# A fused adaLN block on one core: the last attention unit's keys in two halves with a running maximum, and the three-maxima mode from step 101 instead of 121

## The chip, the cores and the metric

The kernel runs on one core of a Trainium2 chip. The metric is the device time of one execution in microseconds (us): the median of three runs is 1090.26 us, and the runs lie between 1089.8 and 1090.3. The profile is of one more execution, which took 1090.18 us; its span, from the first profiled instruction to the last, is 1088.4 us. The engines are named as in the profile: PE (TensorE) multiplies matrices, DVE (VectorE) reduces and does elementwise work, ACT (ScalarE) does exponentials and copies, POOL (GpSimd) does elementwise work, and SP issues most DMAs.

## The reference, cut to what matters

```python
h = _layernorm(x) * (1 + ca) + sa
qkv = (h @ wqkv).reshape(B, S, 3, 16, 28)          # S = 2048, D = 448
scores = einsum("bhqd,bhkd->bhqk", q, k) * scale
p = softmax(scores)
x = x + ga * ((einsum("bhqk,bhkd->bhqd", p, v) -> B,S,D) @ wo)
h = _layernorm(x) * (1 + cb) + sb
x = x + gb * (gelu(h @ w1 + b1) @ w2 + b2)         # F = 1792
```

The weights are scaled up (wqkv and wo by 8, the MLP's by 64), so the scores are large: exp needs the row's maximum taken off first, and products are made of a rounded high part and a low part of each operand (three matmuls: high by high, low by high, high by low).

## The kernel before

**Tiling.** Four groups `g` of four heads by four blocks `qt` of 512 queries make 16 units `u = 4 * g + qt`. A unit has 16 steps, one for each 128 keys `kt`; `step = 16 * u + kt` runs from 0 to 255 (line 1355 on). In a step PE makes the scores of four heads, 12 matmuls (line 1393) into two PSUM tiles of two heads each; ACT takes exp of each tile (line 1406, two instructions in a step); and PE multiplies the step before's weights by V into the PSUM tile `o` (`av`, line 1348). `o` has one buffer for all units. V has a column of ones, so `o` also gathers the softmax's denominator.

**Maxima.** The row maximum of a unit is made ahead of the unit, from the high parts alone: for each unit 64 matmuls (4 sets of 128 queries, 4 heads, 4 chunks of 512 keys; `max_mm`, line 487), each reduced by DVE (`max_one`, line 492; two at once at line 698). `max_fin` (line 527) reduces the parts to one row maximum, and its `put` (line 535) turns them with a DVE transpose and writes them by four SP DMAs into row 28 of the unit's query tile `qst[u]`, where the first score matmul takes it off through a row of ones in K. All maxima of a unit have to be done by step 12 of the unit before it (`LAST_MAX`, line 34; `finish_max`, line 741). `mxq` holds the maxima still to do, in the units' order.

**Two modes.** Up to step 120 (`RING = 121`, line 35) a step emits 3 or 4 maxima as single matmuls between the score matmuls, and part of them as pairs whose difference goes through ACT (`open_pair` and `close_pair`, line 645 on). From step 121 on, a step emits three: a single one beside the first score tile (`emit_single`) and two with one DVE reduction beside the second (`emit_pair`). The two go into the PSUM tile that the next step's second score tile needs, so that tile waits for DVE's reduction. Once no maxima are left, the score tiles go round over three PSUM tiles (`three`, line 1366). Eight steps (8 to 11 of units 13 and 14, `is_wo`) also carry the output projection of an earlier query block and stay in the older mode.

**What runs beside the last steps.** From step 231 on, DVE and POOL make the second layernorm of block 0 (`ln2_stages`, line 1111; the calls are at lines 1287 to 1290): DVE statistics (lines 210, 211) and scaling (line 227), POOL products (lines 1130, 1131), a second round of statistics, a root on POOL (line 217), and four scalings, each with a short copy (line 1139). In steps 244 to 247 PE transposes the result (line 287) into the PSUM tile `m1`, ACT copies it (line 1198) and DVE makes the low part (line 1199). From step 245 on DVE prepares MLP weights that SP loads into `raw` (lines 1215 to 1228, 1236). At each unit's end ACT copies `o` out (line 1312); then come the denominator's reciprocal and its spread over the rows, with three SP DMAs (`den`, `drec`, `osb`, lines 1053 to 1063), two of which wait for the one ahead of them.

Instructions of one engine, and DMAs of one issuing queue, start in the order in which the program emits them, and each waits for what it needs: nothing is reordered.

## Time and profile before

| what | value |
|---|---|
| median of three runs (lowest, highest) | 1090.26 us (1089.8, 1090.3) |
| the profiled execution: time, span | 1090.18 us, 1088.4 us |
| granted TensorE clock | 1.00 over the span |
| DVE busy | 801.5 us, 74% |
| ACT busy | 696.8 us, 64% |
| POOL busy | 231.9 us, 21% |
| first exp of step 0 starts | 164.3 us into the span |
| last exp of step 255 ends | 790.1 us |

Times in what follows are microseconds from the start of the span of this profiled execution. The 256 steps of attention are found by the exp instructions of line 1406, two for each step. A busy PE says little, since matmuls overlap; a step's length says more.

### The profile page before, as it was taken

The numbers are of one execution on the slowest core, as the hardware profiler recorded it, in microseconds if no ns is written. First come the engines' busy times: TensorE is split into PE (matmuls) and PEld (weight loads), VectorE is DVE, ScalarE is ACT, GpSimd is POOL, SyncE is SP. The second block draws the span as 40 slices with busy tenths as digits, with TensorE's granted clock in tenths as the row PEclk, the third lists the DMA queues.
The fourth block names the chain that finished last, engine by engine and source line by source line (L and its number), as shares of the span: only waits on it lengthen the run. The fifth ranks groups of instructions, "written<-read, shape, count | busy, mean of one in ns | idle before, by whom it ended". The sixth has DMA issues, their size and how long they took to land.

```text
span 1088.4 us, 20665 instructions
## 1 busy us (share of the span) xinstructions
PE 1080.0 (99%) x8231; PEld 658.8 (61%) x8231; DVE 801.5 (74%) x1369; ACT 696.8 (64%) x883; POOL 231.9 (21%) x215
## 2 busy tenths in 40 slices
PE   8999999999999999999999999999999999999998
PEld 6766775444444444444444444544388888888887
DVE  6979788999999989988888988584745565464322
ACT  4665658888888888888888888687943321211211
POOL 1543330011011011024231410216114032061000
PEclk9999999999999999999999999999999999999999
DMA  9342272122121202143322423111343311002000
GB/s 312 134 155 76 86 208 88 41 67 58 50 78 59 77 28 58 56 120 87 103 68 77 131 65 96 58 31 59 117 126 96 102 37 41 33 35 73 34 1 34
DMA packets 58870, 88.56 MB, mean 81 GB/s; under 512 B 13807, under 2 KB 25734, under 8 KB 58762
## 3 DMA queue, kind: packets, MB, share of 16 engines
q1 hardware_dynamic: 58290, 86.51, 25.8%
q8 instruction: 64, 1.05, 0.4%
q10 hardware_dynamic: 148, 0.46, 0.1%
q0 software_dynamic: 336, 0.28, 0.1%
q14 instruction: 32, 0.26, 0.1%
HBM read 59.39 MB, written 29.50 MB: 82 GB/s over the span
## 4 chain that ended last, share of the span: by engine, by line
PE 98%; DMA 1%; DVE 1%; ACT 0%; issue 0%; SPq 0%; ACTq 0%
PE s L1393 24%; PE o L1348 24%; PE m L407 17%; PE pa L407 9%; PE m L487 8%; PE s L1485 3%; PE s L1487 3%; PE s L1486 3%; PE s L487 2%; PE t L1487 1%; PE t L1485 1%; PE t L1486 1%; DMA slot_c<-in_w_mod_dram 1%; PE o L287 1%; DVE mxp L492 0%; PE ma L487 0%
## 5 line engine op out<-in xcount | busy, mean ns | idle before, releaser
L492 DVE TENSOR_REDUCE mxp<-m 128x1 f32<-128x512 f32 x553 | 358.1, 686 | 65.0 <-PE m L487 47.7
L1393 PE MATMUL s<-slot_b,slot_a 28*128 28x512 f32 (+1 forms) x3072 | 357.8, 425 | 0.0
L1393 PEld LDWEIGHTS s<-slot_b,slot_a 28*128 28x128 f32 (+1 forms) x3072 | 210.7, 183 | 175.5 <-ACT slot_c L1406 96.4
L487 PE MATMUL m<-kh,qh 28*128 28x512 f32 x606 | 225.8, 469 | 0.8 <-DVE mxp L492 0.3
L1406 ACT ACTIVATE slot_c<-s 128x1024 f32<-128x1024 f32 x170 | 174.8, 1028 | 51.5 <-PE s L1393 50.5
L1348 PE MATMUL o<-slot_c,v 128*32 128x512 f32 x680 | 178.8, 605 | 0.0
L1441 ACT ACTIVATE full<-m,b_col 128x512 f32<-128x512 f32 x56 | 38.6, 690 | 194.2 <-PE m L407 190.0
L698 DVE TENSOR_REDUCE mxp<-s 128x2 f32<-128x1024 f32 x107 | 131.2, 1226 | 5.0 <-PE s L1393 0.3
L1348 PE MATMUL o<-slot_c1h,v 128*32 128x512 f32 x512 | 134.7, 605 | 0.0
L1348 PE MATMUL o<-slot_c0h,v 128*32 128x512 f32 x508 | 133.6, 605 | 0.0
L1406 ACT ACTIVATE slot_c0h<-s 128x1024 f32<-128x1024 f32 x127 | 130.7, 1029 | 0.0
L1406 ACT ACTIVATE slot_c1h<-s 128x1024 f32<-128x1024 f32 x128 | 130.7, 1021 | 0.0
L1406 ACT ACTIVATE slot_d<-s 128x1024 f32<-128x1024 f32 x86 | 88.4, 1028 | 26.1 <-PE s L1393 25.8
L487 PEld LDWEIGHTS m<-kh,qh 28*128 28x128 f32 x606 | 90.4, 182 | 15.4 <-DVE mxp L492 12.7
L1444 DVE CAST hi<-full 128x512 fp32r<-128x512 f32 x42 | 19.2, 458 | 102.0 <-ACT full L1441 101.9
L1068 POOL TENSOR_TENSOR osb<-osb,osb 128x512 f32<-128x512 f32 x16 | 20.6, 1285 | 343.6 <-DMA osb<-drec 282.3
L1348 PE MATMUL o<-slot_d,v 128*32 128x512 f32 x344 | 90.5, 605 | 0.4 <-ACT osb L1312 0.4
L1445 DVE TENSOR_TENSOR lo<-full,hi 128x512 fp32r<-128x512 f32 x56 | 46.2, 825 | 29.7 <-ACT hi L1444 25.7
L407 PE MATMUL m<-y,slot_a 128*128 128x512 f32 x160 | 59.7, 389 | 0.0
L662 DVE CUSTOM_DVE_ANT_0 slot_d0i<-m,slot_d0i 128x512 f32<-128x512 f32 x55 | 38.0, 691 | 16.6 <-PE m L487 14.3
L1348 PEld LDWEIGHTS o<-slot_c,v 128*32 128x32 f32 x680 | 24.5, 108 | 39.7 <-issue 37.8
L492 DVE TENSOR_REDUCE mxp<-ma 128x1 f32<-128x512 f32 x61 | 39.5, 681 | 11.6 <-PE m L487 7.2
(358 smaller groups left out, 1847.1 us busy)
## 6 DMA issues: line engine op xcount, KB each, us to landing
slot_b<-d SPq DMA_DIRECT2D x32, 256.0 KB
slot_a<-d SPq DMA_DIRECT2D x32, 256.0 KB
d<-lo SPq DMA_DIRECT2D x28, 256.0 KB
d<-hi SPq DMA_DIRECT2D x16, 256.0 KB
osb<-drec SPq DMA_DIRECT2D x15, 256.0 KB
out_dram<-xn SPq DMA_DIRECT2D x16, 224.0 KB
raw<-in_B_w_dram SPq DMA_DIRECT2D x14, 224.0 KB
qh<-d SPq DMA_DIRECT2D x12, 256.0 KB
```

Of the source, the lines that this page charges most:

```text
L407: pe.matmul(p, a, b, start=(i == 0), stop=(i == len(terms) - 1))
L487: pe.matmul(m, qh_sb[(g, qt)][js, i * 128 : (i + 1) * 128], k[js, :], start=True, stop=True)
L492: dve.tensor_reduce(out=mxp[(g, qt)][:, i, j, cch : cch + 1], in_=m, op=ALU.max, axis=AX.X)
L698: dve.tensor_reduce(out=mxp[(g, qt)][:, i, j : j + 2, cch], in_=t, op=ALU.max, axis=AX.X)
L1348: pe.matmul(o[32 * j : 32 * j + 32, :], v_sb[kt // 4][:, kt % 4, 4 * g + j, :], p[j // 2][:, j % 2, :], start=(kt == 0), stop=(kt == NKT - 1),
L1393: pe.matmul(s2[:, jj, :], ks[rows_, kp, kc], qs[rows_, qp, :], start=(term == 0), stop=(term == 2))
L1406: act.activation(pt[hf], s2, AF.Exp, scale=SCALE)
L1441: act.activation(gf, p, AF.Gelu_apprx_tanh, bias=b1_col[:, i : i + 1])
L1445: dve.tensor_tensor(out=glo, in0=gf, in1=f(ghi), op=ALU.subtract)
L1485: pe.matmul(pp, ghi[:, ts], w_hi, start=(m == 0), stop=False)
L1486: pe.matmul(pp, ghi[:, ts], w_lo, start=False, stop=False)
L1487: pe.matmul(pp, glo[:, ts], w_hi, start=False, stop=(m == NFT - 1))
```

## The change

Three things are done. `RING` goes from 121 to 101: twenty more steps run in the three-maxima mode. The last unit (`SPLIT`, unit 15) takes its keys in two halves: the maxima over its first 1024 keys are due where all were due before, those over the other 1024 keys by step 3 of the unit itself (`LAST_HALF`, step 243). The second half's score matmuls subtract a second row, the second maximum less the first, so the two halves have their own scale; the sum over the first half is set aside (`o1`), multiplied by exp of the difference of the maxima, and added at the end. For that `shift_exp` makes the factor on ACT and spreads it over the rows by five SP DMAs; a DVE copy empties `o` behind key step 7; POOL multiplies at step 252; and the unit's end adds on DVE where ACT copied. A buffer for descriptors is set to 8192 bytes. The maxima stay 1024 in all, the score and value matmuls the same in number.

```diff
-RING = 121
+RING = 101
+SPLIT = (NG - 1, NB - 1)
+HALF = NKT // 2
+LAST_HALF = NKT * (NG * NB - 1) + 3
...
+    w_dr = dr.tile([4, 512], F32, tag="w_dr", name="w_dr", bufs=1)
+    shift = {}
...
-    def max_fin(g, qt):
+    def max_fin(g, qt, cchs=slice(0, 4), row=0):
...
+        if row:
+            dve.tensor_tensor(out=m32[:, 0:16], in0=f(m32)[:, 0:16], in1=f(shift["m1"])[:, 0:16], op=ALU.subtract)
+        elif (g, qt) == SPLIT:
+            shift["m1"] = m32
         def put():
             r = sbt("full", [128, 512], F32R, bufs=3)[:, :32]
             dve.transpose(f(r), f(m32))
-            dst = f(qst[g * NB + qt])[DH:128:32, 0, :].rearrange("j (i b q) -> j i b q", b=4, q=32)
+            dst = by_block(f(qst[g * NB + qt])[DH + row : 128 : 32, 0, :])
             for b in range(4):
                 sp.dma_start(dst[:, :, b, :], f(r)[32 * b : 32 * b + 16, :])
+            if row:
+                shift["r"] = r
+                at(clock[0], shift_exp)
...
+    def shift_exp():
+        e = sbt("e32", [128, 32])
+        act.activation(e, f(shift["r"]), AF.Exp, scale=SCALE)
+        for b in range(4):
+            sp.dma_start(by_block(w_dr)[:, :, b, :], e[32 * b : 32 * b + 16, :])
+        shift["w"] = sbt("w1b", [128, 512])
+        sp.dma_start(shift["w"], w_dr[:, None, :].broadcast_to([4, 32, 512]))
...
+    def o_shift():
+        pool.tensor_tensor(out=shift["o"], in0=shift["o"], in1=shift["w"], op=ALU.mult)
+    at(last0 + 12, o_shift)
...
-        act.copy(o_sb, o)
+        if u < NU - 1:
+            act.copy(o_sb, o)
+        else:
+            dve.tensor_tensor(out=o_sb, in0=o, in1=shift["o"], op=ALU.add)
...
-                start=(kt == 0), stop=(kt == NKT - 1),
+                start=(kt == 0 or (u, kt) == (NU - 1, HALF)), stop=(kt == NKT - 1 or (u, kt) == (NU - 1, HALF - 1)),
...
+                if (pu, pkt) == (NU - 1, HALF - 1):
+                    shift["o"] = sbt("o1", [128, 512])
+                    dve.tensor_copy(shift["o"], po)
...
-            if kt == 0:
+            if kt == 0 or (u, kt) == (NU - 1, HALF):
                 o = ps_o()
...
-    nc = bacc.Bacc("TRN2", target_bir_lowering=False, num_devices=1)
+    nc = bacc.Bacc("TRN2", target_bir_lowering=False, num_devices=1, dynamic_dma_scratch_size=8192)
```

Left out of the diff are the bookkeeping of the two halves (`count`, `ready_max`, `finish_max`, `extra`) and the second subtracted row in the score matmul's slice (`n_shift`).

**PE, step 104.** The step in the order before and after: `s0`, `s1`, `s2` are the two-head PSUM tiles, `m1` and `m2` the single ones, `kh` and `qh` the high parts from which maxima are made. Before:

```order
L1393 MATMUL s1_1446_5852<-slot_b0_1242_5040,slot_a2_964_3930 128x512 x2
L487 MATMUL m2_1447_5855<-kh3_1185_4808,qh1_922_3767 128x512
L1393 MATMUL s1_1446_5852<-slot_b0_1242_5040,slot_a2_964_3930 128x512 x2
L487 MATMUL m1_1448_5860<-kh3_1185_4808,qh1_922_3767 128x512
L1393 MATMUL s1_1446_5852<-slot_b0_1242_5040,slot_a2_964_3930 128x512 x2
L1393 MATMUL s0_1449_5866<-slot_b0_1242_5040,slot_a2_964_3930 128x512 x6
L487 MATMUL m2_1450_5873<-kh2_1181_4788,qh1_922_3767 128x512
L487 MATMUL m2_1451_5876<-kh2_1181_4788,qh1_922_3767 128x512
```

After (line numbers are those of the changed kernel):

```order
L1444 MATMUL s1_1436_5836<-slot_b0_1242_5041,slot_a2_964_3931 128x512 x2
L490 MATMUL m1_1437_5839<-kh3_1185_4809,qh1_922_3768 128x512
L1444 MATMUL s1_1436_5836<-slot_b0_1242_5041,slot_a2_964_3931 128x512 x4
L1444 MATMUL s0_1438_5847<-slot_b0_1242_5041,slot_a2_964_3931 128x512 x4
L490 MATMUL s2_1439_5852<-kh2_1181_4789,qh1_922_3768 128x512 x2
L1444 MATMUL s0_1438_5847<-slot_b0_1242_5041,slot_a2_964_3931 128x512 x2
```

Four maxima matmuls in the step have become three, two of them into one tile and inside the second score group. Steps 101 to 120 all change in this way (their 79 maxima matmuls become 60). The 20 matmuls that leave steps 99 to 120 come back in steps 234 (one more), 235 (three, before none), 236 to 240 (three each, before none) and 241 (one).

**DVE, steps 237 and 238.** The layernorm's statistics (`st`, `mv`) and scaling (`xn`) of block 0, before:

```order
L210 BN_STATS st_10398<-xn_10320 128x6
L211 BN_AGGR mv_10397<-st_10398 128x2
L227 TENSOR_SCALAR xn_10401<-acc_17_101,mv_10137,rs_10281 128x448
L210 BN_STATS st_10427<-xn_10371 128x6
L211 BN_AGGR mv_10397<-st_10427 128x2
L227 TENSOR_SCALAR xn_10430<-acc_17_101,mv_10137,rs_10281 128x448
```

After:

```order
L495 TENSOR_REDUCE mxp_9655<-m_2398_10291 128x1
L733 TENSOR_REDUCE mxp_9655<-s_2400_10304 128x2
L213 BN_STATS st_10316<-xn_10230 128x6
L214 BN_AGGR mv_10315<-st_10316 128x2
L230 TENSOR_SCALAR xn_10319<-acc_17_101,mv_10030,rs_10182 128x448
L495 TENSOR_REDUCE mxp_9655<-m_2407_10328 128x1
L733 TENSOR_REDUCE mxp_9655<-s_2409_10341 128x2
L213 BN_STATS st_10352<-xn_10282 128x6
L214 BN_AGGR mv_10315<-st_10352 128x2
L230 TENSOR_SCALAR xn_10355<-acc_17_101,mv_10030,rs_10182 128x448
```

Each step's two reductions now stand ahead of its layernorm work. The same holds in steps 236, 239 and 240. Behind the last scaling of step 242 now stands the transpose of the second row, and behind the weights' third item (`raw`, step 247) the copy of `o`.

**SP, steps 242 to 246.** Before, from the loads of the first two weight rows:

```order
L1215 DMA raw_10551<-in_B_w_dram 128x512
L1215 DMA raw_10553<-in_B_w_dram 128x512
L1061 DMA drec_10616<-den_10522 128x16
L1063 DMA osb_10618<-drec_10616 128x1x512
L1215 DMA raw_10653<-in_B_w_dram 128x512
```

After:

```order
L1250 DMA raw_10495<-in_B_w_dram 128x512
L1250 DMA raw_10497<-in_B_w_dram 128x512
L553 DMA slot_b_2302_9846<-full_10499 4x4x32 x4
L564 DMA w_dr<-e_2449_10528 16x32 x4
L566 DMA w1b_10534<-w_dr 128x1x512
L1096 DMA drec_10574<-den_10466 128x16
L1098 DMA osb_10576<-drec_10574 128x1x512
L1250 DMA raw_10611<-in_B_w_dram 128x512
```

Nine DMAs have come ahead of unit 14's reciprocal and of the load of the third weight row, and three of the waits in this queue are now for landings that did not exist before or for DVE and ACT work of steps 242 and 243.

More of the change, by code (lines that the diff above doesn't have):

```diff
@@ L586, in count @@
                     load_hi(1, g + 1, cch)
-        if left[(g, qt)] == 0:
+        if (g, qt) == SPLIT:
+            before = first_left[0]
+            first_left[0] -= sum(cch < 2 for cch in cchs)
+            if before and not first_left[0]:
+                max_fin(g, qt, slice(0, 2))
+            if left[(g, qt)] == 0:
+                max_fin(g, qt, row=1)
+        elif left[(g, qt)] == 0:
             max_fin(g, qt)
@@ L607, in ready_max @@
     def ready_max():
-        return [m for m in mxq if there(1, m[0], m[2]) and there(0, *m[:2])][: 24 if clock[0] >= RING else 64]
+        near = [m for m in mxq if there(1, m[0], m[2]) and there(0, *m[:2])][: 24 if clock[0] >= RING else 64]
+        if near and clock[0] >= RING and NKT * (near[0][0] * NB + near[0][1] - 1) + LAST_MAX <= clock[0] + 8:
+            near = [m for m in near if m[:2] == near[0][:2] and (m[:2] != SPLIT or m[2] < 2 or not first_left[0])]
+        return near
     def by_set(m):
@@ L1331, in extra @@
         need = 0
[L1332 to L1334 removed]
+        ends = [(NKT * (v - 1) + LAST_MAX, left.get(divmod(v, NB), 64)) for v in range(s_ // NKT + 1, NU - 1)]
+        if s_ < NKT * (NU - 2) + LAST_MAX:
+            ends.append((NKT * (NU - 2) + LAST_MAX, first_left[0]))
+        if s_ < LAST_HALF:
+            ends.append((LAST_HALF, left.get(SPLIT, 64) - first_left[0]))
+        for end, n in ends:
+            need += n
+            rest = range(s_, end)
             n_wo = sum(is_wo(x) for x in rest)
```

19 lines of the change are left out of this document (11 added, 8 removed).

## The prediction

> **What bounds the kernel now.** I read the page's busy times and its chain of waits first.
>
> ```profile
> span 1088.4 us, 20665 instructions
> PE 1080.0 (99%) x8231; PEld 658.8 (61%) x8231; DVE 801.5 (74%) x1369; ACT 696.8 (64%) x883; POOL 231.9 (21%) x215
> ...
> PE 98%; DMA 1%; DVE 1%; ACT 0%; issue 0%; SPq 0%; ACTq 0%
> ```
>
> PE carries the chain from end to end and waits for almost nothing, so time is won only where a PE stretch gets shorter and lost wherever PE begins to wait. A busy PE does not tell how much it does, so the next view is the length of steps: windows over the exp instructions of line 1406, two to a step, each window from the end of one step's first exp to the end of a later step's first (the two exps cut by the edges are counted too).
>
> ```profile
> core 0: us, ACT busy (x), PEclk, DMA share, GB/s
> 419.66:469.90 50.24, 38.90 (x42) 1.00 0.19 58
> 521.70:557.80 36.10, 31.05 (x34) 1.00 0.35 101
> 748.77:756.75 7.98, 7.76 (x10) 1.00 0.20 78
> ```
>
> The first window is steps 101 to 120 in the older mode: 50.24 / 20 = 2.51 us a step. The second is the 16 steps of unit 9 in the three-maxima mode: 36.10 / 16 = 2.26. The third is steps 236 to 239, without maxima: 7.98 / 4 = 2.00. The clock is 1.00 in all three. So three maxima cost PE 0.26 us in the newer mode, 0.087 each, since they run beside score matmuls in other rows of the array.
>
> **Part 1, steps 101 to 120.** They go from 2.51 to 2.26 us: 20 x 0.256 = 5.1 us less; step 99 drops one matmul, which makes it **-5.2**. Nothing else moves to these steps. DVE does two reductions in place of three or four, and steps 121 to 233 keep their three maxima each.
>
> **Part 2, the twenty maxima that come back in steps 234 to 241.** On PE alone they cost 20 x 0.087 = 1.7 us. But DVE has the second layernorm to do there. Its timeline gives start, duration, line and tiles, and in brackets the idle time ahead and who ended it:
>
> ```profile
> start us, us, engine line op out<-in xcount [idle before <-releaser]
> 726.94 0.69 DVE L492 TENSOR_REDUCE mxp<-m 128x1 f32<-128x512 f32 x1 [0.34 <-PE m L487]
> 727.62 1.23 DVE L698 TENSOR_REDUCE mxp<-s 128x2 f32<-128x1024 f32 x1
> 728.76 0.62 DVE L210 BATCH_NORM_STATS2 st<-acc 128x6 f32<-128x448 f32 x1
> 729.41 0.18 DVE L211 BATCH_NORM_AGGREGATE mv<-st 128x2 f32<-128x6 f32 x1
> 729.51 1.85 DVE L492 TENSOR_REDUCE mxp<-m 128x1 f32<-128x512 f32 x3
> ...
> 751.24 0.63 DVE L210 BATCH_NORM_STATS2 st<-xn 128x6 f32<-128x448 f32 x1 [3.37 <-POOL xn L1131]
> 751.90 0.18 DVE L211 BATCH_NORM_AGGREGATE mv<-st 128x2 f32<-128x6 f32 x1
> 752.00 0.56 DVE L227 TENSOR_SCALAR xn<-acc,mv,rs 128x448 f32<-128x448 f32 x1
> ...
> 755.92 0.63 DVE L210 BATCH_NORM_STATS2 st<-xn 128x6 f32<-128x448 f32 x1 [1.48 <-POOL xn L1131]
> ...
> 756.80 0.17 DVE L215 TENSOR_SCALAR ve<-mv 128x4 f32<-128x4 f32 x1
> 758.10 1.33 DVE L227 TENSOR_SCALAR xn<-xn,mv,rs 128x448 f32<-128x448 f32 x1 [1.13 <-POOL rs L217]
> ...
> 763.42 0.51 DVE L227 TENSOR_SCALAR xn<-xn,mv,rs 128x448 f32<-128x448 f32 x1
> 763.96 0.20 DVE L1139 COPY xn<-xn 128x64 f32<-128x64 f32 x1
> ```
>
> Queued without a pause, instructions overlap a little: a single reduction takes 0.61 (1.85 for three) and a double one 1.14 (727.62 to 728.76), so a step's three maxima are 1.75 us of DVE. The layernorm work behind them is, by step: 236 a scaling, 0.5; 237 and 238 statistics and a scaling, 751.24 to 752.56 less the overlap, 1.24 each; 239 statistics, 0.84 (751.24 to 752.08); 240 the same and `ve`, 1.05 (755.92 to 756.97). That is 4.9, and with 5 x 1.75 it is **13.6 us of DVE in five steps** for which PE alone would take 11.3. Today DVE idles there and waits for POOL (the 3.37 and 1.48 in brackets). Afterwards POOL's two products of 1.15 each end well inside a DVE step of 3 us, and DVE is what is late. PE feels it directly: the second score tile of a step is the one that the step before's double reduction must have emptied.
>
> When does DVE start and what waits for its end? PE's timeline:
>
> ```profile
> 747.68 0.62 PE L1348 MATMUL o<-slot_c,v 128*32 128x512 f32 x2
> ...
> 765.14 0.66 PE L287 MATMUL m<-ident,xn 128*128 128x128 f32 x4
> ...
> 776.23 0.62 PE L1348 MATMUL o<-slot_c,v 128*32 128x512 f32 x2
> ```
>
> The scores of step 236 stand just ahead of the matmul of 747.68, so its first reduction can begin about 747.9, and 748.2 with the four maxima more of steps 234 and 235 (4 x 0.087). Add 13.6: `ve` ends at 761.8, where it ended at 756.97. The root on POOL takes 1.13 until DVE goes on (756.97 to 758.10), beside which the last single maximum and the two small operations on maxima fit: 763.0. The four last scalings and copies took 758.10 to 764.16, 6.06 us: 769.0. The new transpose adds 0.2, by the grouped rows of DVE (count, busy us, mean ns):
>
> ```profile
> L537 DVE STREAM_TRANSPOSE full<-m 128x32 f32<-128x32 f32 x1 | 0.2, 203 | 0.0
> ```
>
> So the second row is turned at 769.2. Two things hang on this. The first transposes of step 244 need all four scaled rows; they ran at 765.14, one microsecond behind DVE. And ACT's queue now holds `e32`, the exp of the turned row, ahead of the exps of step 244 (ACT's timeline):
>
> ```profile
> 764.24 1.02 ACT L1406 ACTIVATE slot_c<-s 128x1024 f32<-128x1024 f32 x1
> ...
> 791.42 0.20 ACT L1440 ACTIVATE full<-cst 128x1 f32<-128x1 f32 x1
> ```
>
> With `e32` at the price of the small activation of 0.20, step 244's exps start at 769.45 where they started at 764.24: **+5.2**. From there ACT has two exps of 1.02 and a copy in each step of 2.5 us, no room to catch up, so everything behind is later by that. This contains the 1.7 of PE. Bounds: 1.92 a step without overlap gives +6.1. If the last scalings ran at the 0.51 and 0.20 of their final pair, 2.8 in place of 6.06, it would be +1.9, little over PE's own price, and the sum 3.3 less.
>
> On that stretch a rule can be weighed. POOL's four additions lie beside it:
>
> ```profile
> 758.04 4.76 POOL L1161 TENSOR_TENSOR acc<-acc,row_b2g 128x448 f32<-128x448 f32 x4
> ```
>
> The scaling of 1.33 lies inside them, the one of 0.51 behind them. The Trainium skill, SBUF — State Buffer, section Who interferes with whom, says that a DVE operation in a two-port mode and a GpSimd operation take turns at a shared pair of ports, and the later one is fully blocked. The trace agrees (1.33 against 0.51). By the rule the stretch keeps its 6.06, since the additions again follow the root at once.
>
> **Part 3, the set-aside of `o`.** `o` has one buffer, so the first value matmul of the second half (step 249, 776.23 above) now waits for the DVE copy of `o`. In DVE's queue that copy stands behind the cast of the third weight row, and that row's load stands on SP behind nine new DMAs. The prices, from the timelines of SP and of DVE:
>
> ```profile
> 717.87 0.32 SPq L1061 DMA_DIRECT2D drec<-den  x1
> 720.40 0.54 SPq L1063 DMA_DIRECT2D osb<-drec  x1
> ...
> 742.67 2.27 SPq L540 DMA_DIRECT2D slot_b<-full  x4
> ...
> 767.56 0.33 SPq L1061 DMA_DIRECT2D drec<-den  x1
> 769.02 0.55 SPq L1063 DMA_DIRECT2D osb<-drec  x1
> 769.62 0.47 SPq L1215 DMA_DIRECT2D raw<-in_B_w_dram  x1
> ```
>
> ```profile
> 774.20 0.69 DVE L1199 TENSOR_TENSOR y<-m,y 64x512 fp32r<-64x512 f32 x1 [0.75 <-ACT y L1198]
> 775.30 1.18 DVE L1227 CAST slot_b<-raw 128x512 fp32r<-128x512 f32 x1 [0.40 <-DMA raw<-in_B_w_dram]
> 776.51 0.98 DVE L1228 TENSOR_TENSOR slot_a<-raw,slot_b 128x512 fp32r<-128x512 f32 x1
> ```
>
> From the turn at 769.2: four row DMAs 2.27, 771.5; four of `w_dr` between 0.33 and 0.57 each, taken as 0.45, 773.3; the wait for the last one's landing, 1.46 from its issue as for `drec` (767.56 to 769.02), 774.3; `w1b` 0.55, 774.9; `drec` and its landing, 776.4; `osb`, then the third row's load at 777.0. Its landing took 769.62 to 775.30, 5.68, with a broadcast just ahead as it has here: 782.6. Cast and difference 1.18 + 0.98, and the copy 0.69 (a 128x512 tile read from PSUM, as in the row of 774.20): 785.5. The matmul would be ready at 776.23 + 5.2 = 781.4. **+4.1.** Bounds: landing as fast as `drec`, 1.46, gives no wait at all; both write landings at the 2.5 of 717.87 to 720.40 and 0.57 for each `w_dr` give 6.7. I take the row of the very same load.
>
> The Trainium skill, DMA: Bandwidth & Descriptors, section Anatomy of one DMA, gives about 2.0 us of fixed cost to a DMA, for another issuing path than SP's. The trace shows 1.46 and 2.5 here. By the page's figure the two write landings would take 1.1 more together, an estimate, and the sum would be 1095.4.
>
> The rest costs nothing that PE sees. The second row lands by 773 and is needed at step 248, after 778: five microseconds of cover, and if it failed the price would be what it lacks. The factor's product on POOL and the addition at the end lie in front of a long MLP; DVE's addition takes the place of ACT's copy. The smaller descriptor buffer concerns three POOL DMAs behind the last step, which have the MLP as cover; I put it at 0, with at most a microsecond of SP-like issue time beside PE.
>
> **The sum.** -5.2 + 5.2 + 4.1 = +4.1 on the profiled 1090.18 (the median is 1090.26, 0.1 away): **1094.3 us**.
>
> **Rivals.** *The copy of `o` is in time* (the load lands in 1.5 us, or the chain on SP is shorter): -5.2 + 5.2, 1090.2, no change. It decides at a load that lands by 778.5. For it: the load is only 256 KB. Against it: 5.68 in the same place. *The layernorm doesn't hold PE, and the copy is in time, too*: only PE's 1.7 is paid, -5.2 + 1.7, 1086.7, **faster**. The mechanism is the last scalings running free of POOL's additions: then DVE turns the row near 766, where PE with 1.7 of delay arrives at 766.8 (765.14 + 1.7). It decides at 2.2 us less on DVE between 748 and 769. For it: each pair costs 0.71 when alone. Against it: the additions follow the root in POOL's queue. If only this half holds and the copy is late, it is 1090.8. *The change doesn't do what it says*: steps 101 to 120 stay at 2.51 because units 6 and 7 wait for loads that unit 9 did not: 1099.5. Against it: the score tiles, the queues and the number of maxima of a step are the same there as in unit 9.
>
> **How the numbers follow.** Chances: forecast 0.45, copy in time 0.25, both covered 0.18, only the scalings covered 0.07, no gain 0.05. The forecast's own range, with copy waits from 1.5 to 6.7, is 1091.7 to 1097. The range given, 1087.0 to 1097.0, takes in the cases of no change and half of the faster one; it leaves out the rest of that, the no-gain case and the upper tail, under 0.2. A measurement tells 0.2%, 2.2 us, from no change: faster 0.22 (both covered, and a part of the second case), same 0.30, slower 0.48.
>
> **What would show it.** Step length near 2.26 in steps 101 to 120 (part 1). In steps 236 to 240, DVE without idle time and PE's second score tile released by the double reduction; steps near 3 us (part 2). A PE gap ahead of step 244's transposes, released by DVE, and ACT idle ahead of `e32`. At step 249 a PE gap at the first value matmul, released by the DVE copy, with that DVE waiting for `raw`'s DMA (part 3). The prediction is wrong if the layernorm's scalings end within 2 us of where they ended, counted from step 236, or if step 249 has no gap.

## The result, and the profile after

The changed kernel takes **1100.34 us** (median of five runs, 1099.78 to 1101.9), the kernel before took 1089.95 beside it: a ratio of 1.0097, 95% interval 1.0083 to 1.0111. The forecast was 1094.3 in a range of 1087.0 to 1097.0: the sign was right, the size was less than half of what came. Ranges and intervals, here and below, leave out two executions that took far longer than all others of their kernel, 1942.88 us of `both` and 1618.89 us of the kernel before beside both_adds, both_exp and best2. The profiled execution of the change took 1100.62 us. From its page, the span, the busy times, the slices of PE and of its granted clock (40 slices of 27 us), and the chain of waits:

```profile
span 1098.8 us, 20650 instructions
PE 1081.7 (98%) x8231; PEld 657.1 (60%) x8231; DVE 809.7 (74%) x1350; ACT 692.6 (63%) x873; POOL 232.8 (21%) x216
...
PE   8999999999999999999999999999799999999998
PEclk9999999999999999999999999999899999999999
...
PE 96%; DMA 2%; DVE 1%; ACT 1%; issue 0%; SPq 0%; ACTq 0%
```

The busy times hardly moved. One slice stands out: the 29th, where PE is at 7 and its clock at 8. It lies at 769 to 797 us, the last steps of attention. To see where the time goes, take from ACT's timeline of each trace the end of every step's first exp, and subtract:

| end of the first exp of step | before, us | after less before, us | what lies between |
|---|---|---|---|
| 101 | 419.69 | -0.38 | |
| 121 | 469.90 | -5.49 | part 1: -5.1 |
| 198 | 644.71 | -5.45 | |
| 200 | 649.14 | -4.16 | +1.3, not foreseen |
| 234 | 739.84 | -4.30 | |
| 240 | 756.79 | -2.49 | part 2, first half: +1.8 |
| 244 | 765.26 | -0.17 | part 2, second half: +2.3 |
| 249 | 777.19 | -0.39 | part 2 in all: +3.9 |
| 250 | 779.26 | +9.23 | part 3: +9.6 |
| 251 | 781.19 | +10.53 | part 3 in all: +10.9 |
| 255 | 789.19 | +10.53 | |

The span differs by 10.44. Part 1 is there: windows over the exps, cut as in the prediction, give 45.13 / 20 = 2.26 us a step in steps 101 to 120 (2.51 before). The second window is steps 236 to 239, 2.40 us a step where they took 2.00.

```profile
419.28:464.41 45.13, 38.86 (x42) 1.00 0.21 65
744.70:754.30 9.60, 7.88 (x9) 1.00 0.17 66
```

Part 2 on DVE: the first reduction of step 236, `ve`, the first of the four scalings and the turn of the second row. POOL's additions (the last line, from POOL's timeline) run beside the scalings:

```profile
743.21 0.69 DVE L495 TENSOR_REDUCE mxp<-m 128x1 f32<-128x512 f32 x1 [2.26 <-PE m L490]
...
756.43 0.17 DVE L218 TENSOR_SCALAR ve<-mv 128x4 f32<-128x4 f32 x1
...
757.74 1.34 DVE L230 TENSOR_SCALAR xn<-xn,mv,rs 128x448 f32<-128x448 f32 x1
...
763.70 0.21 DVE L550 STREAM_TRANSPOSE full<-m 128x32 f32<-128x32 f32 x1
```

```profile
757.67 4.75 POOL L1196 TENSOR_TENSOR acc<-acc,row_b2g 128x448 f32<-128x448 f32 x4
```

Part 3 begins on SP. Its timeline after the turn of the second row (start, duration, tiles, count):

```profile
763.94 2.26 SPq L553 DMA_DIRECT2D slot_b<-full  x4
766.30 1.79 SPq L564 DMA_DIRECT2D w_dr<-e  x4
769.14 0.56 SPq L566 DMA_DIRECT2D w1b<-w_dr  x1
769.80 0.42 SPq L1096 DMA_DIRECT2D drec<-den  x1
774.35 0.55 SPq L1098 DMA_DIRECT2D osb<-drec  x1
774.95 0.47 SPq L1250 DMA_DIRECT2D raw<-in_B_w_dram  x1
```

`osb` reads what `drec` wrote, so SP waits for `drec`'s landing: 769.80 to 774.35, 4.55 us, where the same pair took 1.46 before. DVE's and PE's timelines show the rest, the cast that waits for the row, the copy behind it, and the value matmul that waits for the copy:

```profile
780.80 1.33 DVE L1262 CAST slot_b<-raw 128x512 fp32r<-128x512 f32 x1 [6.29 <-DMA raw<-in_B_w_dram]
782.16 0.98 DVE L1263 TENSOR_TENSOR slot_a<-raw,slot_b 128x512 fp32r<-128x512 f32 x1
783.17 0.69 DVE L1467 COPY o<-o 128x512 f32<-128x512 f32 x1
```

```profile
783.91 1.07 PE L1396 MATMUL o<-slot_c,v 128*32 128x512 f32 x2 [8.01 <-DVE o L1467]
```

The matmul takes 1.07 us where it took 0.62. Windows tell why (length; busy time and count of PE, PEld, DVE, ACT, POOL; then the granted clock, the share of the DMA engines and GB/s):

```profile
770.00:776.00 6.00, 5.91 (x60) 2.67 (x58) 2.99 (x5) 5.83 (x8) 0.00 (x0) 1.00 0.17 52
776.00:779.95 3.95, 0.00 (x0) 0.00 (x0) 0.00 (x0) 1.71 (x2) 0.00 (x0) 1.00 0.83 223
780.05:790.20 10.15, 6.29 (x36) 2.13 (x40) 9.13 (x13) 1.94 (x2) 4.94 (x4) 0.50 0.39 128
790.30:792.00 1.70, 1.70 (x22) 0.58 (x18) 1.63 (x4) 1.31 (x2) 0.00 (x0) 1.00 0.77 248
```

Four us into PE's idle time the granted clock falls to 0.50, and it stays there for 10.2 us, 6.3 of them after PE has begun again. Half of 6.3 is 3.1 us of lost clock, close to the 2.9 that steps 249 to 251 lost beside the 8.0 of waiting (10.9 less 8.0).

The +1.3 at step 198 goes with a wait of PE for DVE that the kernel before doesn't have there:

```profile
639.38 0.50 PE L490 MATMUL s<-kh,qh 28*128 28x512 f32 x1 [0.78 <-DVE mxp L495]
```

Three single reductions follow one another there; `emit_pair` found no two neighbours among the few maxima that the new rule in `ready_max` leaves it close to a due time.

### The profile page after: what moved, and what is told of

Read it like the earlier page. It is cut to its first block, busy times and chain, and to the rows that moved or that the text cites. A ratio compares the mean times of both kernels' runs of the same rounds, so it can differ in the third digit from the quotient of the medians.

```text
span 1098.8 us, 20650 instructions
## 1 busy us (share of the span) xinstructions
PE 1081.7 (98%) x8231; PEld 657.1 (60%) x8231; DVE 809.7 (74%) x1350; ACT 692.6 (63%) x873; POOL 232.8 (21%) x216
## 4 chain that ended last, share of the span: by engine, by line
PE 96%; DMA 2%; DVE 1%; ACT 1%; issue 0%; SPq 0%; ACTq 0%
PE s L1444 24%; PE o L1396 23%; PE m L410 16%; PE pa L410 9%; PE m L490 7%; PE s L1539 3%; PE s L1541 3%; PE s L1540 3%; PE s L490 2%; PE t L1541 1%; PE t L1539 1%; PE t L1540 1%; DMA slot_c<-in_w_mod_dram 1%; PE o L290 1%; DVE mxp L495 1%; DMA raw<-in_B_w_dram 1%
## 5 line engine op out<-in xcount | busy, mean ns | idle before, releaser
L495 DVE TENSOR_REDUCE mxp<-m 128x1 f32<-128x512 f32 x523 | 340.6, 686 | 72.9 <-PE m L490 55.2
L1444 PE MATMUL s<-slot_b,slot_a 28*128 28x512 f32 (+2 forms) x3072 | 358.7, 426 | 0.1
L1444 PEld LDWEIGHTS s<-slot_b,slot_a 28*128 28x128 f32 (+2 forms) x3072 | 211.4, 184 | 186.9 <-ACT slot_c L1457 106.2
L490 PE MATMUL m<-kh,qh 28*128 28x512 f32 x566 | 215.5, 470 | 0.8 <-DVE mxp L495 0.3
L733 DVE TENSOR_REDUCE mxp<-s 128x2 f32<-128x1024 f32 x131 | 160.6, 1226 | 5.8 <-PE s L1444 0.5
L490 PEld LDWEIGHTS m<-kh,qh 28*128 28x128 f32 x566 | 85.5, 182 | 13.3 <-DVE mxp L495 10.7
L490 PE MATMUL s<-kh,qh 28*128 28x512 f32 x264 | 59.0, 438 | 0.8 <-DVE mxp L495 0.8
```

Source lines behind the costliest of these rows:

```text
L490: pe.matmul(m, qh_sb[(g, qt)][js, i * 128 : (i + 1) * 128], k[js, :], start=True, stop=True)
L495: dve.tensor_reduce(out=mxp[(g, qt)][:, i, j, cch : cch + 1], in_=m, op=ALU.max, axis=AX.X)
L733: dve.tensor_reduce(out=mxp[(g, qt)][:, i, j : j + 2, cch], in_=t, op=ALU.max, axis=AX.X)
L1444: pe.matmul(s2[:, jj, :], ks[rows_, kp, kc], qs[rows_, qp, :], start=(term == 0), stop=(term == 2))
```

## The experiments

Thirteen kernels, each beside the kernel before on the same chip. "Gap" is PE's idle time ahead of step 249's first value matmul.

| kernel | median, us (lowest, highest) | ratio to before, interval | gap, us |
|---|---|---|---|
| the change | 1100.34 (1099.78, 1101.9) | 1.0097 [1.0083, 1.0111] | 8.0 |
| copy_first | 1097.22 (1096.94, 1099.31) | 1.0067 [1.0054, 1.0080] | none |
| spread_late | 1095.45 (1094.46, 1095.94) | 1.0044 [1.0029, 1.0060] | 3.2 |
| split_only | 1096.34 (1094.47, 1097.11) | 1.0053 [1.0039, 1.0067] | 1.9 |
| ring_only | 1098.07 (1097.71, 1099.39) | 1.0074 [1.0062, 1.0087] | none |
| both | 1090.64 (1089.39, 1093.7) | 1.0005 [0.9996, 1.0014] | none |
| pool_queue | 1095.03 (1094.49, 1095.58) | 1.0043 [1.0029, 1.0057] | 3.9 |
| keep_busy | 1099.17 (1098.2, 1100.11) | 1.0081 [1.0067, 1.0095] | 1.0 |
| best1 | 1089.42 (1088.23, 1090.41) | 0.9991 [0.9982, 1.0000] | none |
| both_adds | 1090.62 (1089.22, 1091.82) | 1.0003 [0.9994, 1.0013] | none |
| both_exp | 1090.0 (1089.12, 1091.52) | 1.0001 [0.9992, 1.0010] | none |
| best2 | 1088.24 (1087.45, 1088.72) | 0.9982 [0.9973, 0.9991] | none |
| spray_w1b | 1098.56 (1097.31, 1099.61) | 1.0082 [1.0067, 1.0097] | 7.0 |
| spray_both | 1096.8 (1096.26, 1097.95) | 1.0070 [1.0053, 1.0087] | 4.9 |

**copy_first: the copy ahead of the late cast.**

```diff
-        at(last0 + 5 + k + (k >= 4), w_prep.step)
+        at(last0 + 5 + k + (k >= 2), w_prep.step)
```

> The changed kernel, with the weight preparation's third and fourth items one step later each (steps 248 and 249 in place of 247 and 248), so that the DVE copy of o stands ahead of the cast that waits for the late weight load. Theory: the wait at step 249 is the copy standing behind that cast, and the slow TensorE clock of the next steps comes from PE's idle time. Then the 8.0 us gap and the 2.8 us of slow clock go: 1100.3 - 10.9 = 1089.4 us, granted clock 1.00 throughout. Rival 1: the late load itself holds PE, if not there then where the weights are first used: the time stays above 1097 us with a new gap near 790 us. Rival 2: the slow clock has another cause: the gap goes and the time is about 1092.3 us.

The gap at step 249 is gone: the offset against before is +0.6 from step 245 to step 255. But the time is 1097.22, not the 1089.4 of the theory. Most of the loss came back some 20 us later, in the MLP's projection, as PE's timeline shows (the profiled execution, 1099.31, is the slowest of the five; the others lie below 1097.3):

```profile
800.75 0.44 PE L410 MATMUL m<-slot_e,slot_c 128*128 128x448 f32 x1 [3.22 <-DMA slot_c<-o]
803.22 0.71 PE L410 MATMUL m<-slot_e,slot_c 112*128 112x448 f32 x1 [2.03 <-DMA slot_c<-o]
```

Behind the first of these waits the granted clock is 0.50 again, from 802.7 to 809.4. SP issues the loads of `slot_c` at 797.35; before it did at 789.34. So removing the wait at PE doesn't heal the queue that was late: it moves the wait to the next reader of that queue. The rival had this mechanism, if with other loads.

**spread_late: the broadcast of `w1b` five steps later**, behind `drec` instead of ahead of it.

```diff
+        at(clock[0] + 5, shift_spread)
+
+    def shift_spread():
         shift["w"] = sbt("w1b", [128, 512])
```

> The changed kernel, with the spread of the factor over the rows (the broadcast DMA into w1b) issued at step 248, behind the weight loads, in place of step 243. Theory: drec's landing took 4.55 us from its issue because the broadcast was in the DMA queues ahead of it. Then it takes about 1.5 us, the third weight row's load is issued 3.6 us earlier (3.05 for the landing and 0.6 for the broadcast's issue), and PE's gap at step 249 goes from 8.0 to about 4.4 us: 1096.7 us if the clock falls as before, about 1094 us if the shorter gap keeps it. Rival: drec's landing is slow for another reason, and it stays near 4.5 us: 1099.7 us.

SP's timeline: from `drec`'s issue to `osb`'s are 1.48 us now, not 4.55.

```profile
768.67 0.37 SPq L1099 DMA_DIRECT2D drec<-den  x1
770.15 0.56 SPq L1101 DMA_DIRECT2D osb<-drec  x1
```

The gap fell from 8.0 to 3.2 (forecast 4.4), and still cost 5.85 in steps 249 to 251: the clock's price, 2.7, stayed.

**both: the two edits together.**

> Both single edits together: the set-aside copy of o stands ahead of the casts of the third weight row, and the broadcast of w1b is issued in step 248 instead of behind w_dr. Theory (all of the late loss comes from SP's queue: the copy behind a late cast, and drec's landing behind the broadcast's packets): the reciprocal's DMA lands in about 1.2 us instead of 4.5, the gap of 8.0 us ahead of step 249's value matmuls is gone as in copy_first, and the projection's loads (slot_c<-o) come early enough that the gaps of 3.2 and 2.0 us near 800 are gone too; what is left is -5.1 +1.3 +3.9 = about 0, so 1089 to 1091. Rival (the eight small DMAs of SP, four slot_b and four w_dr, make the tail's loads late by themselves): gaps of 2 to 5 us near 795 to 805 stay, 1093 to 1096.

It came out nearly as the theory had it: `drec` to `osb` 1.50 us (forecast 1.2), no gap at step 249, none near 800, and a span 0.3 us under that of before. Part 3 is thus two things together: SP's queue, late behind the broadcast, and the copy's place on DVE behind the cast that waits for SP's load (split_only, below, has the second alone). What is left is -5.1 + 1.3 + 3.9 = 0.1. The smaller descriptor buffer was not tried alone, but from step 255 (-0.23) to the end of the span (-0.3) `both` loses nothing, so the prediction's 0 for it holds here.

**split_only and ring_only: one part of the change alone.** split_only leaves `RING` at 121; ring_only is the kernel before with `RING = 101`.

> The changed kernel with RING back at 121: the split of the last unit without the longer three-maxima mode. All maxima are done by step 234, as before the change; the second row is turned about step 235, and its nine DMAs are through before unit 14's reciprocal. Theory: nothing of the layernorm is held up, and the third weight row lands as it did before the change; what is left is the copy of o behind its cast: 775.3 + 1.18 + 0.98 + 0.69 = 778.2 where the matmul could start at 776.2, a gap of 2 us: 1092 us. Rival: the split itself (its nine DMAs, the second row, the extra DVE and POOL work) costs more by itself: 1094 us or above.

> The kernel before with RING at 101 and nothing else: the last unit isn't split, and 20 steps between 108 and 227 carry a fourth maximum to keep the old due time. Theory: steps 101 to 120 give 5.1 us, and the fourth maximum costs what a step of the older mode costs over one of the newer, 0.25 us, since DVE then has about 2.4 us of reductions in a step of 2.26: 20 x 0.25 = 5.0 us, 1089.9 us, no change. Rival: a fourth maximum costs PE's 0.087 us alone, 1.7 us in all: 1086.5 us, faster, and the split was not needed for the gain.

split_only has no late maxima, since they are made by step 234, and its offset stays at +1.0 from step 235 to 249, so part 2's loss needs the late maxima. It took 1096.34 where its theory had 1092. The theory's gap is there (1.86 us, forecast 2), but two terms were not in it. At step 212 three single reductions stand in a row again, PE waits 0.78 us for DVE, and the offset goes from -1.0 to +1.0 by step 215. And the clock drops even for a gap of 1.86, 1.3 us after PE has begun again and for 3.4 us (windows as above):

```profile
779.15:780.49 1.34, 1.34 (x12) 0.47 (x16) 1.31 (x2) 0.00 (x0) 1.34 (x2) 1.00 0.60 171
780.49:783.90 3.41, 3.41 (x24) 1.08 (x20) 3.31 (x6) 1.94 (x2) 0.43 (x1) 0.50 0.40 120
783.90:785.00 1.10, 1.10 (x20) 0.35 (x12) 1.07 (x3) 0.39 (x1) 0.00 (x0) 1.00 1.06 401
```

Its median lies 1.9 us above its profiled execution; that difference is not explained. ring_only shows what the split is for: without it the twenty maxima must come back by step 235. In the trace sixteen of them are a fourth one in a step (108, 116 and fourteen steps from 124 to 227), and the other four stand in steps 234 and 235. Its offset goes from -2.96 at step 121 to +8.86 at step 231, 11.8 / 14 = 0.84 us for each, where the theory had 0.25 and the rival 0.087: both failed. One of PE's waits for DVE there:

```profile
619.05 0.50 PE L487 MATMUL m<-kh,qh 28*128 28x512 f32 x1 [0.85 <-DVE mxp L492]
```

**pool_queue: the nine DMAs on POOL's queue.**

```diff
-                sp.dma_start(dst[:, :, b, :], f(r)[32 * b : 32 * b + 16, :])
+                (pool if row else sp).dma_start(dst[:, :, b, :], f(r)[32 * b : 32 * b + 16, :])
...
-            sp.dma_start(by_block(w_dr)[:, :, b, :], e[32 * b : 32 * b + 16, :])
+            pool.dma_start(by_block(w_dr)[:, :, b, :], e[32 * b : 32 * b + 16, :])
...
-        sp.dma_start(shift["w"], w_dr[:, None, :].broadcast_to([4, 32, 512]))
+        pool.dma_start(shift["w"], w_dr[:, None, :].broadcast_to([4, 32, 512]))
```

> The change as it is, but the second row's four DMAs, the four of w_dr and the broadcast of w1b are issued by POOL instead of SP; the copy of o stays behind the cast. Theory (it is their place in SP's queue that makes the third weight row, its cast, the copy and the projection's loads late): SP is in time as before, drec's landing about 1.5 us, the gap ahead of step 249's value matmuls under 1 us, no lower granted clock behind it, no gaps near 800: about 1090.2 (-5.1 +1.3 +3.9). Rival 1 (the landing of drec is slow because the broadcast's packets load the DMA engines, whatever queue they come from): drec still lands 3 us or more later than it was issued, the gap at step 249 stays at 2 to 4 us and the clock drops: 1094 to 1096. Rival 2 (POOL, which waits for e32 and then issues, holds its own copies and scalings): new waits on POOL's tiles, over 1094 without a wait for osb.

SP is in time (`drec` to `osb` 1.44 us, the third row's load issued at 767.54), and yet a gap of 3.9 us stays. Gap and time are those of the first rival, but its late `drec` is not there. POOL waits 5.20 us for `w_dr`, and its own work then falls on DVE's cast (DVE's timeline, then POOL's):

```profile
773.32 3.19 DVE L1262 CAST slot_b<-raw 128x512 fp32r<-128x512 f32 x1 [0.36 <-DMA raw<-in_B_w_dram]
776.55 0.98 DVE L1263 TENSOR_TENSOR slot_a<-raw,slot_b 128x512 fp32r<-128x512 f32 x1
777.56 0.69 DVE L1467 COPY o<-o 128x512 f32<-128x512 f32 x1
```

```profile
773.14 0.71 POOL L566 DMA_DIRECT2D w1b<-w_dr  x1 [5.20 <-DMA w_dr<-e]
773.86 1.15 POOL L1196 TENSOR_TENSOR acc<-acc,row_b2g 128x448 f32<-128x448 f32 x1
774.96 1.26 POOL L1103 TENSOR_TENSOR osb<-osb,osb 128x512 f32<-128x512 f32 x1
```

Such a cast takes 0.42 at 770.37, while POOL waits, and this one 3.19 beside three instructions of POOL. The theory missed this; the second rival had the place (POOL held up) but not the way in which it cost.

The run also bears on part 2, by accident. POOL makes only two of its four additions before it comes to the new DMAs, and DVE's scalings are short as soon as those two end (POOL's timeline, then DVE's):

```profile
757.19 2.39 POOL L1196 TENSOR_TENSOR acc<-acc,row_b2g 128x448 f32<-128x448 f32 x2
```

```profile
757.25 1.33 DVE L230 TENSOR_SCALAR xn<-xn,mv,rs 128x448 f32<-128x448 f32 x1
...
759.56 0.50 DVE L230 TENSOR_SCALAR xn<-xn,mv,rs 128x448 f32<-128x448 f32 x1
```

The stretch of scalings is 4.4 us instead of 6.05, the second row is turned in time for `e32`, which waits for nothing, and between steps 242 and 244 nothing is lost (-2.09 to -2.06).

**keep_busy: matmuls in the gap.** 64 score matmuls that nothing reads stand ahead of step 249's value matmuls.

```diff
+                if (pu, pkt) == (NU - 1, HALF):
+                    busy = ps_s2()
+                    for n in range(64):
+                        rows_ = slice(32 * (n % 2), 32 * (n % 2) + DH)
+                        pe.matmul(busy[:, n % 2, :], ks[rows_, 0, kc], qs[rows_, 0, :], start=n < 2, stop=n >= 62)
```

> The change as it is, and 64 more matmuls of the score form into a free score buffer just ahead of step 249's value matmuls, in place of part of the 8.0 us wait (by the rows of step 251, where a pair starts every 0.2 us, they take about 6.4 us); nothing reads them. Theory (the granted clock falls because PE idles for 8 us): the wait left is about 1.6 us, the windows behind it show a granted clock near 1.0, the value matmuls of step 249 take 0.62 us instead of 1.07, steps 249 to 251 are 2 to 3 us shorter and the time falls to 1097 to 1098.5 although PE does more. Rival (the clock falls for another reason, such as the matmuls' own load): the value matmuls stay near 1.07 us and the time stays at 1100.3 or goes over it.

PE's timeline and the window behind the gap:

```profile
785.03 0.62 PE L1396 MATMUL o<-slot_c,v 128*32 128x512 f32 x2 [0.96 <-DVE o L1472]
```

```profile
784.00:788.00 4.00, 3.04 (x32) 0.89 (x30) 3.90 (x6) 0.96 (x2) 2.80 (x2) 1.00 0.20 57
```

The clock is 1.00, the value matmuls take 0.62, and steps 249 to 251 lose 8.6 us instead of 10.9, though PE does more. The time fell by 1.2 only, to 1099.17 where the forecast was 1097 to 1098.5; in the profiled pair 0.6 went to a later start of step 0 (+0.1 against -0.5). That idling is what takes the clock is shown.

**both_adds and both_exp: what part 2's second half is.** both_adds moves POOL's additions four stages later in the program, both_exp moves `e32` to step 248 (and the broadcast to 249, its use to 253).

```diff
-                (t, 4 + t, 6 + t, 10 + t // 2, 10 + t),
+                (t, 4 + t, 6 + t, 10 + t // 2, 14 + t),
```

```diff
-                at(clock[0], shift_exp)
+                at(clock[0] + 4, shift_exp)
```

> both, and POOL's additions to block 0 four stages later (t of 14 to 17 instead of 10 to 13), nothing else. Theory A (in steps 242 to 244 the loss comes from DVE's scalings and copies that run beside POOL's additions and are three times as long): the stretch of scalings shrinks from 6.06 us to 2.8 to 4.7 and the offset against before at step 244, 0.0 in both, falls to -1.3 to -2.0: 1088.5 to 1089.2. Theory B (the loss comes from e32, which holds ACT's queue until the second row is turned, whatever the scalings last): the offset at step 244 stays within 0.4 of both's and the time at 1090.5.

> both, and e32 with its w_dr DMAs four steps later (step 248), the broadcast in step 249 and its use in step 253, nothing else. Theory A (long scalings beside POOL's additions hold DVE; ACT waits because it is behind them): e32 no longer holds ACT, but PE then waits for DVE itself or not at all: offset at step 244 from 0.0 to -0.3 at most if DVE was what PE waited for. Theory B (only e32's place on ACT makes a late turn of the row cost anything): the stretch of scalings stays at 6.06 us, the offset at step 244 falls by 1.3 us or more: about 1089.

both_adds moved nothing on the chip. POOL has nothing else to do there, so it reaches the additions at the same time as before, and DVE's scaling is as long as ever (POOL's timeline, then DVE's):

```profile
757.91 1.02 POOL L220 TENSOR_TENSOR rs<-ve,cst 128x4 f32<-128x4 f32 x1 [2.78 <-DVE ve L218]
758.90 4.76 POOL L1199 TENSOR_TENSOR acc<-acc,row_b2g 128x448 f32<-128x448 f32 x4
```

```profile
758.96 1.34 DVE L230 TENSOR_SCALAR xn<-xn,mv,rs 128x448 f32<-128x448 f32 x1
```

So it says nothing on theory A; pool_queue, above, does. both_exp settles the other side: between steps 242 and 244 the offset moves by 0.0 (-1.36 to -1.35) where `both` lost 1.5 (-1.46 to 0.00), with the scalings as long as they were. So the 1.5 us need both: the long scalings, which turn the second row late, and `e32`'s place in ACT's queue, which holds the exps until then. pool_queue takes away the first, both_exp the second, and either is enough. The time doesn't show the gain: the span of both_exp is 1088.2 us, that of `both` 1088.1, because the projection, whose loads of `slot_c` SP issues no earlier (790.67 against 790.48), gives back what steps 242 to 244 won; the forecast of about 1089 was missed by 1.0. The other 2.7 us (-4.06 at step 234 to -1.36 at step 242 in both_exp) stay. split_only, without the late maxima, loses nothing there; best2, below, with the layernorm moved away, still loses 1.2, near the 1.7 that the prediction had for the maxima on PE alone. So some 1.5 of the 2.7, by the difference of best1 and best2, are DVE's, which carries late maxima and layernorm together. In the change the row of `e32` was:

```profile
763.94 0.23 ACT L562 ACTIVATE e<-full 128x32 f32<-128x32 f32 x1 [1.31 <-DVE full L550]
```

**spray_w1b and spray_both: why a small DMA lands late behind a broadcast.** In the change, the DMA view of 771 to 773 us, when only `w1b`'s packets run (busy tenths of the 16 DMA engines in 40 slices, then packets, MB and share):

```profile
DMA  2142222332232323313323143132331431323314
...
q1 hardware_dynamic: 97, 0.20, 26.0%
```

Only a quarter of the engines is busy, and of `drec`'s 128 packets 96 had gone by 770.9 while 32, a quarter, came at 773.1 to 773.7. The edit makes one DMA for each of the four source rows; spray_both does the same for unit 14's `osb`, just ahead of the third weight row.

```diff
-        sp.dma_start(shift["w"], w_dr[:, None, :].broadcast_to([4, 32, 512]))
+        for j in range(4):
+            sp.dma_start(shift["w"][32 * j : 32 * j + 32, :], w_dr[j][None].broadcast_to([32, 512]))
```

> The change as it is, but the broadcast of w1b is four DMAs, one for each row of w_dr onto 32 partitions, instead of one whose source has 4 rows of 32 copies. Theory (the one broadcast runs on 4 of the 16 DMA engines, since 32 of drec's 128 packets, 4 engines' share of 16, came 2.4 us after the other 96; drec waits for those four): the packets of w1b spread over all engines and last about 0.8 us instead of 3.1, drec lands in 1.5 us or less instead of 4.5; SP issues 1.1 us more, so the third weight row is about 2 us earlier and the gap ahead of step 249's value matmuls falls from 8.0 to 5.5 to 6.5, the clock still drops: 1098 to 1099. Rival (any 256 KB in the same queue holds a small DMA behind it, on however many engines): drec lands as late as before, and with SP's 1.1 us more the gap grows to 9: 1101.5.

> spray_w1b, and unit 14's broadcast of the reciprocal (osb<-drec, just ahead of the third weight row's load) is four DMAs in the same way. Theory: the load of the third weight row lands in 2.5 to 3 us instead of 5.85, because the four engines are no longer busy with the broadcast; SP issues another 1.2 us more; the gap at step 249 falls to 3.5 to 4.5 us, the clock still drops: 1096 to 1097. Rival (the 5.85 us are the load's own, or all DMA engines are full there): landing stays over 5 us and the gap grows against spray_w1b by the 1.2 us of issue: about 1100.

SP's timeline in spray_w1b: the broadcast is still right ahead of `drec`, and `osb` follows `drec` by 1.83 us instead of 4.55.

```profile
769.71 2.00 SPq L567 DMA_DIRECT2D w1b<-w_dr  x4
771.75 0.42 SPq L1097 DMA_DIRECT2D drec<-den  x1
773.58 0.56 SPq L1099 DMA_DIRECT2D osb<-drec  x1
```

In spray_both the third weight row lands 2.95 us after its issue (6.22 in spray_w1b, 5.85 in the change), by SP's and DVE's timelines:

```profile
775.32 0.42 SPq L1255 DMA_DIRECT2D raw<-in_B_w_dram  x1
```

```profile
778.27 0.43 DVE L1267 CAST slot_b<-raw 128x512 fp32r<-128x512 f32 x1 [4.07 <-DMA raw<-in_B_w_dram]
```

Both times came as forecast; the gaps were 7.0 and 4.9, some 0.5 over the forecast, and the four issues took 2.0 and 2.6 us. So these broadcasts occupy four engines, and whatever has a share on those four waits behind it. The Trainium skill, DMA: Bandwidth & Descriptors, section Why a DMA increments its semaphore by 16 and not by 1, states that rule: the number of engines is the largest up to 16 that divides the slowest dimension of both sides, here 4. The trace agrees (26.0%, and 32 packets of 128).

**best1 and best2: versions meant to beat both kernels.** best1 has copy_first's edit, the later additions, `e32` at step 248, the broadcast at 249, its use at 253, and the near rule at 4 steps instead of 8. best2 also moves block 0's layernorm off the late maxima:

```diff
-        if near and clock[0] >= RING and NKT * (near[0][0] * NB + near[0][1] - 1) + LAST_MAX <= clock[0] + 8:
+        if near and clock[0] >= RING and NKT * (near[0][0] * NB + near[0][1] - 1) + LAST_MAX <= clock[0] + 4:
...
-                (t, 4 + t, 6 + t, 10 + t // 2, 14 + t),
+                (t, 8 + t, 10 + t, 14 + t // 2, 20 + t),
...
-        at(last0 + 4 + k, lambda k=k: lnst[0][1](k))
+        at(last0 + 8 + k, lambda k=k: lnst[0][1](k))
```

> The change with five edits: copy of o ahead of the third weight row's casts; POOL's additions to block 0 four stages later, so that DVE's scalings in steps 234 to 241 don't meet them; exp of the shift (e32) and its w_dr DMAs four steps later, in step 248, the broadcast of w1b in step 249, the use of it in step 253; and the planner's rule for near due times from 4 steps ahead instead of 8, which leaves no step of three single reductions (198 had one). Theory: -5.1 from steps 101 to 120 stays, +1.3 of step 198 goes, the stretch of scalings falls from 6.06 us to about 2.8 and with it the loss of steps 234 to 244 from 3.9 to 1 to 2, no gap at step 249 and none near 800: 1086 to 1087.5, faster than before. Rival 1 (SP's queue stays late in the tail because e32's DMAs now fall among the tail's weights): gaps of 2 to 5 us near 795 to 805, 1089 to 1092. Rival 2 (DVE's slowness in steps 234 to 241 is layernorm's and the reductions' alone): loss there still 3.5 to 4, 1088.5 to 1089.5.

> best1, and block 0's second layernorm put out of the steps with late maxima: the first scaling four stages later (steps 239 to 242 instead of 235 to 238), its second statistics in 241 to 244, the last scaling in 245 and 246, POOL's additions in 251 to 254, the transposes of the normalised block in 248 to 251. Theory (the loss of 2.7 us between steps 235 and 244 that best1 still has is DVE carrying layernorm beside three maxima a step): the offset against before, -5.4 at step 234, is still -4.5 to -5.2 at step 244; the work that is moved lies beside 1.93 us steps whose DVE share is low, so it costs nothing there: 1085.5 to 1087.0. Rival 1 (the reductions alone are too much, since three maxima in 2.26 us need two reductions of 1.92 us in a row and a step of the last unit has less time): loss still over 2, 1088 to 1089. Rival 2 (the moved transposes and scalings delay the copy of o or the casts of the weights): a gap over 1 us at step 249 or near 790 to 800, 1089 to 1093.

best1: no loss at step 198 (offset -5.49 there, -5.48 at step 200), no gaps, but 2.7 between steps 235 and 244 instead of 1 to 2. Its additions moved as little as in both_adds, so that term of its forecast fell away. The median is 1089.42, above the forecast, and with an interval that ends at 1.0000 it isn't told from before. best2: the loss from step 235 to 244 falls to 1.2 (-5.34 to -4.15; the forecast was -4.5 or lower), and -3.95 is left at step 252, behind the moved transposes. The projection takes another 1.6, part of it by a small gap (the span is 2.4 under that of before):

```profile
794.09 0.44 PE L410 MATMUL m<-slot_e,slot_c 112*128 112x448 f32 x1 [0.89 <-DMA slot_c<-o]
```

Its 1088.24 is over the forecast of 1085.5 to 1087.0, but it is the fastest here: 0.18% under the kernel before, interval 0.9973 to 0.9991, and 1.1% under the change.

## Why the prediction was wrong in size

**Part 1, -5.2: right.** Measured -5.1, at 2.26 us a step and a clock of 1.00.

**"Steps 121 to 233 keep their three maxima each": true, but not enough.** The number was kept, the form was not: step 198 makes three single ones. It cost 1.3 us, a term that the sum doesn't have, and the order of step 198, shown nowhere in the prediction, would have told it.

**Part 2, +5.2: right in mechanism, 1.3 too large.** Steps near 3 us came only in 239 and 240 (2.9 each); 236 to 238 took 2.1 to 2.3. DVE ran without idle time from step 236 on; its work from the first reduction at 743.21 to the end of `ve` at 756.60 took 13.4 us (13.6 forecast); the root and what lies beside it 1.1 (1.2), the scalings 6.05 (6.06). They stayed long beside POOL's additions, in agreement with the Trainium skill, SBUF — State Buffer, section Who interferes with whom. The term mis-sized is the start: 743.21 is 747.3 on the time scale of before (4.1 us added, the offset at step 236), not 748.2. The last 0.2 was caught up between steps 244 and 249, where the prediction saw no room. `e32` held ACT by 1.31 us, as forecast, but PE's transposes did not wait for DVE, which the prediction named as a second way. That the first two parts come to 0.1 together, where the forecast had 0.0, is luck: step 198's 1.3 happens to be what part 2 was too large by.

**Part 3, +4.1: right in mechanism, less than half in size.** Two terms failed. The first was "its landing, 1.46 from its issue as for `drec`": that row is of a `drec` with no broadcast ahead of it. From the turn of the row to the weight row's load the forecast has 7.8 us, measured 11.0; of the 3.2 more, 3.1 are this landing. The second isn't in the sum at all: PE's wait was priced at its own length, and it costs the clock, too, 2.9 us. The row's load itself, 5.68 forecast from a row with the same broadcast ahead of it, took 5.85; spray_both shows that this broadcast is what makes it long (2.95 with it split).

A rule that speaks of the second term was at hand and not weighed. The Trainium skill, TensorE: Matmul & The Clock Gate, section What's actually happening, says that PE's clock is halved after an idle window of about 3.4 us and restored after as long a busy one. The forecast wait of 4.1 us was over that. The trace agrees in the half clock (0.50) and in that length (3.4 us at 0.50 in split_only, two and three times as long in other runs), but not in the threshold: a wait of 1.86 us took the clock to 0.50, one of 0.96 did not.

**The sum.** -5.1 + 1.3 + 3.9 + 10.9 = 11.0, forecast -5.2 + 5.2 + 4.1; the span's difference of 10.44 has in it a start that was 0.5 earlier. The rival "the copy is in time" was what `both` made: it forecast 1090.2, and 1090.64 came. "The rest costs nothing" was false in one place: once the copy is in time, SP's late queue delays the projection's loads (copy_first).

## What to carry to other kernels

Price a DMA's landing from a row with the same neighbours in its queue: a broadcast from four rows sits on four engines, and a small DMA behind it waits for all of it. A wait of PE of 1.9 us or more cost more than its length here, since the clock fell with it; and when such a wait is taken away, look for the next reader of the queue that was late. Moving an instruction later in the program of an idle engine moved nothing (both_adds): see first what else would hold it back.

## What the runs showed of the hardware

A PE wait of 1.86 us was followed by a granted clock of 0.50, one of 0.96 us was not; beside their own length the waits of 1.9, 3.2, 3.9, 4.9, 7.0 and 8.0 us cost 1.6, 2.7, 2.7, 1.8, 2.6 and 2.9 us until step 251. The price does not go by the length of the wait but by how much of the stretch at 0.50 lies behind it. That stretch was 3.4 us in split_only, 6.8 in spread_late, pool_queue and spray_both and 10.2 in spray_w1b and the change; of it 3.4, 5.8, 5.8, 3.8, 5.7 and 6.3 us lay behind the wait, in the order above, and half of each is within 0.3 of the price. A DVE cast of 0.42 us took 3.19 beside POOL's elementwise work. And a broadcast of 256 KB from four source rows kept a quarter of the DMA engines busy for 3.1 us, where four DMAs of one row each ended 2.3 us after the first packet (770.67 to 772.98) with an issue of 2.0 us.
